# Letting the last routing steps of a top-2 mixture-of-experts kernel run on into the second expert block

## The chip, the cores and the metric

One core of one Trainium2 chip runs the kernel. The metric is the device time of one execution in microseconds; three runs are given, with their median. One further execution was taken with the hardware profiler.

## What is computed

Local attention over 64-token chunks (8 batches, 8 heads, 576 tokens, head size 64) gives 4608 tokens of 512 features. Each token then goes to the two best of eight experts, chosen by noisy logits:

```python
scores = scale * np.matmul(q_c, k_c.transpose(0, 1, 2, 4, 3))
attn = softmax(scores)                     # within each chunk of 64
x = heads_joined(np.matmul(attn, v_c))     # 4608 x 512
noisy_logits = x @ w_gate + np.log1p(np.exp(x @ w_noise)) * noise
top2_w = softmax of the two largest noisy logits
for e in range(8):
    h = np.maximum(x[mask] @ w1[e], 0.0)   # 512 -> 1024
    out[mask] += top2_w[mask, k, None] * (h @ w2[e])
```

All of it is in float32.

## The kernel before, in words

The program's order on each engine is the order in which the Python code issues instructions (`manual_schedule`); nothing reorders it. Each engine works through its own list and waits on semaphores where an operand is not ready.

**Attention and routing.** 36 tiles of 128 tokens go through attention (`attend`). Their results are written to `xbuf` in DRAM. The tiles form five groups, and for each group `route(g)` works out the two experts of every token, its place in each expert's list, and adds the group's share to the lists. `route` is a generator: it issues some instructions and yields, and `step_route(n)` lets it go on by n yields. So routing is woven between other work. `finish_route` (L614) issues all that is left at once.

For each of the eight tiles of a group, `route` builds comparison matrices (`gohp` on GpSimd, L557, and ScalarE, L558 and L559; `geq` and `grhs` on VectorE, L561 and L565 for the last group) and `place` (L547, matmuls on L549) sums their product into one PSUM bank. A tile's two `place` matmuls are called a pair here. Three buffers of each kind rotate, so a tile's matrices wait for the pair three tiles earlier. When all eight pairs are done, VectorE adds the bank to `acc` (L583), for the last group permutes the sums into the experts' order in four steps of two instructions (L596, L598), and `finish_lists` (L187 to L193, five instructions) makes the row numbers `lid`, the weights `lwt` and a float copy `lfl`. Then `gather(2)` (L601, issued on L219) fetches block 2's tokens with four indirect DMAs on GpSimd's queue.

The experts are put in an order by load; `order` (L522) holds it, and is known before the comparison matrices of the last group are begun. SP loads it into registers (L752) to fetch the later experts' weights (`w_load`).

**Experts.** Each expert's list is cut into three blocks, of 384, 384 and up to 448 tokens. `layer1(i)` makes eight slices f of the hidden layer; each slice is four steps d, and each step three matmuls of 128 x 384 (`three`, L284: hi*hi, hi*lo, lo*hi of float32 split into two parts). ScalarE then makes `hh` (L297) and VectorE `hl` (L298). `layer2(i)` makes, for each tile k of 128 tokens, eight times three matmuls; VectorE weighs the result (L304) and GpSimd adds it to `out` by an indirect DMA (L251). `x_tile` transposes a gathered tile for the next block (L267 on TensorE, hi on ScalarE L274, lo on VectorE L275).

Expert 0 is special: its first two blocks use lists of earlier groups (`EARLY`), so they can start before routing is done. Block 0's first layer still has attention's tail in it. Block 0's second layer takes two routing steps after each f, block 1's too (`hook2_r`), and `finish_route` stands between the two blocks. In block 1's second layer, after the first three matmuls, `pieces` (L197 to L207) turns `lfl` into indices of quarter rows: VectorE writes `xv` (L200), four matmuls (L204) spread the list, VectorE makes `piece` (L206). GpSimd then gathers block 3's tokens in twelve quarters (L239). `pg.close()` gives the routing buffers' memory back, and three pools take it.

Block 2's tiles are transposed within block 1's second layer, the first one after seven f of its first tile.

Of the kernel before, what the change touches and what calls it, by code (L numbers as in the profile page):

```python
# [51 lines left out]
def kernel(ctx, tc, qT, kT, vh, wgn, noise, w1, w2, out, caps=CAPS):  # L52
# [56 lines left out]
    def w_load(e, which, c):  # L109
        st = stage.tile([P, 1024], FT, name="st")  # L110
        staged[e, which, c] = st
        if which == 1:
            nc.sync.dma_start(st, w1v[ds(place[e], 1), c].rearrange("o j r f -> (o j) r f") if e else w1[e, c * P:(c + 1) * P, :])
        else:
            nc.sync.dma_start(st.rearrange("p (f n) -> p f n", f=2),
                              w2[ds(place[e], 1) if e else slice(0, 1), 2 * c * P:(2 * c + 2) * P, :]
                              .rearrange("o (f p) n -> p (o f) n", f=2))

    def w_split(e, which, c, half, eng=None):
        if half == 0:  # L120
            W[e, which, c] = (wpool.tile([P, 1024], FR, name=f"w{which}h{c}"),
                              wpool.tile([P, 1024], FR, name=f"w{which}l{c}"))
        hi, lo = W[e, which, c]
        st = staged[e, which, c]
        s = slice(half * 512, half * 512 + 512)
        nc.scalar.activation(hi[:, s], st[:, s], AF.Copy)
        (eng or nc.vector).tensor_sub(lo[:, s], st[:, s], hi[:, s].bitcast(FT))
# [44 lines left out]
    def bank(what, among=None):  # L172
        among = among or (BANKS if rot["l2"] < 6 else WIDE)[what]
        rot[what] += 1
        return PS[:, among[rot[what] % len(among)], :]
# [67 lines left out]
    def gathered(i, k):  # L243
        while quarters and quarters[0][0:2] <= (i, k):
            gather_some(1)
# [12 lines left out]
    def x_tile(i, k):  # L258
        e, b = BL[i]
        j, r = blocks[e][b][k]  # L260
        xh, xl = XH[i] = BX[i % 2]
        x = XG[e, j]
        s = slice(k * P, k * P + r)
        if i < NPE:
            src = bank("tr").rearrange("p (d n) -> p d n", d=ND)[:, :, 0:r]
            for d in range(ND):
                nc.tensor.transpose(src[:, d, :], x[0:r, d * P:(d + 1) * P], ident[0:r, 0:r])  # L267
            oh, ol = xh[:, :, s], xl[:, :, s]
        else:
            y = xy.tile([P, DM], FT, name="y")  # L270
            nc.vector.transpose(y[:, 0:4 * r], x[:, 0:4 * r])  # L271
            src = y[:, 0:4 * r].rearrange("p (t b c) -> p b t c", b=ND, c=32)
            oh, ol = (a[:, :, s].rearrange("p b (t c) -> p b t c", c=32) for a in (xh, xl))
        nc.scalar.activation(oh, src, AF.Copy)  # L274
        nc.vector.tensor_sub(ol, src, oh.bitcast(FT))  # L275

    def three(p, w, w_s, x, x_s, first, last, flip=False):

        (wh, wl), (xh, xl) = w, x
        for n, (a, b) in enumerate(((wh, xh), (wh, xl), (wl, xh)) if not flip else ((wh, xh), (wl, xh), (wh, xl))):  # L280
            a, b = a[w_s], b[x_s]
            if flip:
                a, b = b, a
            nc.tensor.matmul(p, a, b, start=first and n == 0, stop=last and n == 2)  # L284

    def layer1(i, hook, hook_d=lambda f, d: None):
        e, b = BL[i]
        n = sum(r for _, r in blocks[e][b])
        HT[i] = BH[i % 2]
        for f in range(NF):  # L290
            p = bank("l1", (0, 1) if i == 0 else None)[:, 0:n]
            for d in range(ND):
                three(p, W[e, 1, d], (slice(None), slice(f * P, (f + 1) * P)),
                      XH[i], (slice(None), d, slice(0, n)), d == 0, d == ND - 1)
                hook_d(f, d)
            hh, hl = HT[i][f]
            nc.scalar.activation(hh[:, 0:n], p, AF.Relu)  # L297
            nc.vector.scalar_tensor_tensor(hl[:, 0:n], p, 0.0, hh[:, 0:n].bitcast(FT), op0=OP.max, op1=OP.subtract)  # L298
            hook(f)
# [139 lines left out]
    def route(g):  # L439
# [73 lines left out]
        if g == LAST:  # L513

            key = gate.tile([P, NE], FT, name="gkey")
            V.tensor_copy(key, run8)
            V.memset(key[:, 0:1], float(2 ** 24))
            top = gate.tile([P, NE], FT, name="gtop")
            V.max(top, key)
            idx = gate.tile([P, NE], U32, name="gidx")  # L520
            V.max_index(idx, top, key)
            V.tensor_copy(order, idx[0:1])  # L522
            yield
            perm = gate.tile([P, NE, NE], FT, name="gperm")
            V.tensor_tensor(perm, e_row[:, None, :].to_broadcast([P, NE, NE]),
                            idx[:, :, None].to_broadcast([P, NE, NE]), OP.is_equal)
            accp = gate.tile([P, 2, NJ, NE], FT, name="gaccp")
            by_e = gate.tile([1, NE, NE], FT, name="gbye")
            V.tensor_tensor(by_e, perm[0:1].rearrange("p r e -> p e r"),
                            caprow[:, None, :].to_broadcast([1, NE, NE]), OP.mult)  # L530
            V.tensor_reduce(cape, by_e, AX.X, OP.add)
            yield
# [70 lines left out]
    routing = []  # L603

    def step_route(n):
        for _ in range(n):
            while routing:
                try:
                    next(routing[0])
                    break  # L610
                except StopIteration:
                    routing.pop(0)

    def finish_route():  # L614
        while routing:
            step_route(1)

    halves = [(c, h) for c in range(4) for h in range(2)]
# [79 lines left out]
    for i in range(NBL + 1):  # L698
        e, b = BL[i] if i < NBL else (NE, 0)
        if b == 1 % nb and e + 1 < NE and i > 1:  # L700
            for c in range(4):
                w_load(e + 1, 1, c)
        split2 = halves if i < NBL and (b == 1 % nb if e else b == 0) else []
        nxt = blocks[BL[i + 1][0]][BL[i + 1][1]] if i + 1 < NBL else []

        def turn_next(k):
            gathered(i + 1, k)
            x_tile(i + 1, k)
            ahead[0] -= 1

        def hook1(f):
            if i > 1 and b != 1 and f % 2 == 1 and f // 2 < len(nxt):
                turn_next(f // 2)
            if split2:
                w_split(e, 2, *split2[f])
            if i > 1:
                gather_some(1 + f % 2, HT[i][f][0])

        def hook2_f(k, f):
            if i > 1 and b == 1 and f % 4 == 1 and 2 * k + f // 4 < len(nxt):  # L720
                turn_next(2 * k + f // 4)
            if (k, f) == (0, 3):
                for q in split1:
                    w_split(split1_e, 1, *q)

        def hook2_r(k, f):
            hook2_f(k, f)
            step_route(2)
            if k + 1 < len(nxt) or i == 0:
                if f == 6 and k < len(nxt):  # L730
                    x_tile(i + 1, k)
            if i == 1 and (k, f) == (0, 0):
                pieces()
                gathered(3, 3)

        if 1 < i < NBL and i == 3:
            layer2(i - 1, hook2_f)
        if i < NBL:
            layer1(i, hook1, hook_tail if i == 0 else lambda f, d: None)
        split1 = halves if (i < NBL and b == nb - 1 and e + 1 < NE) else []  # L740
        split1_e = e + 1

        if i == 0:
            pa.close()
            block_bufs(1)
            OB[0] = pb.enter_context(tc.tile_pool(name="ob", bufs=4))
        if i == 0:
            zero_out(NT)
            layer2(0, hook2_r)
            finish_route()  # L750
            for r in range(1, NE):
                place[r] = nc.values_load(order[0:1, r:r + 1], engines=[mybir.EngineType.SP], min_val=0, max_val=NE - 1)  # L752
            for c in range(4):
                w_load(1, 1, c)
            pg.close()
            later_xg.append(pb.enter_context(tc.tile_pool(name="xg2", bufs=3)))
            xy = pb.enter_context(tc.tile_pool(name="xy", bufs=2))
            xv.append(pb.enter_context(tc.tile_pool(name="xv", bufs=1)))
        elif i == 1:
            layer2(1, hook2_r)  # L760
            x_tile(2, 3)
        elif i != 2 and i != 3:
            layer2(i - 1, hook2_f)
        if split1:
            for c in range(4):
                w_load(e + 1, 2, c)
# [132 lines left out]
```

## Time and profile before

| | |
|---|---|
| median of three runs | 1031.76 us (1029.02 to 1033.64) |
| profiled execution | 1033.37 us |
| its span | 1031.5 us |
| mean granted clock of TensorE | 0.981 of 2.4 GHz |
| TensorE / VectorE / ScalarE / GpSimd busy | 95% / 45% / 29% / 46% |

The span is the time from the first to the last instruction in the trace; the execution's own time also has what lies around it. A busy share is a mean over the whole span, in which attention, routing and the experts follow one another. Matmuls are pipelined: a duration of 0.34 us overlaps with the next matmul, so pitches are read from start to start.

### The profile page before, as it was taken

How to read it: one execution, taken by the hardware profiler on the slowest of the kernel's cores; microseconds unless marked ns; L12 is line 12 of the kernel's file. 1: busy time of each engine (PE TensorE's matmuls, PEld its weight loads, DVE VectorE, ACT ScalarE, POOL GpSimd, SP SyncE). 2: the span in 40 equal slices, each digit the busy share in tenths (PEclk: the TensorE clock that was granted, in tenths of full speed). 3: DMA queues.
4: the chain of work that ended last, by engine and by line, in shares of the span. 5: the costliest groups of instructions: out<-in, count | busy, mean ns of one | idle time of the engine just before them, and what ended most of it. 6: DMA issues, size and time to landing. Idle time of an engine off the chain costs nothing.

```text
span 1031.5 us, 17805 instructions
## 1 busy us (share of the span) xinstructions
PE 978.0 (95%) x7121; PEld 866.5 (84%) x7121; DVE 462.0 (45%) x1030; ACT 298.3 (29%) x617; POOL 479.6 (46%) x612
## 2 busy tenths in 40 slices
PE   6778978989999999999999999999999999999995
PEld 5666757887889889888988998899889998999884
DVE  5686665562525443344334432453245334533311
ACT  3565554331314221222222321232123222322100
POOL 1142422445675666157714772378428724801111
PEclk9989888999999999999999999999999999999998
DMA  9987891142442452345224423443334334412213
GB/s 370 402 326 256 280 388 51 41 113 67 95 105 82 95 133 57 58 101 138 54 53 104 130 60 49 103 136 61 51 111 122 77 54 106 135 19 31 31 21 42
DMA packets 51445, 121.48 MB, mean 118 GB/s; under 512 B 8272, under 2 KB 8528, under 8 KB 51360
## 3 DMA queue, kind: packets, MB, share of 16 engines
q0 software_dynamic: 19664, 38.69, 21.7%
q1 hardware_dynamic: 26512, 72.20, 19.3%
q10 hardware_dynamic: 5184, 9.44, 2.4%
q8 instruction: 56, 0.92, 0.4%
q14 instruction: 29, 0.24, 0.1%
HBM read 81.56 MB, written 38.73 MB: 117 GB/s over the span
## 4 chain that ended last, share of the span: by engine, by line
PE 89%; DVE 5%; DMA 2%; ACT 1%; issue 1%; POOL 0%; SPq 0%; ACTq 0%; DVEq 0%; POOLq 0%
PE PS L284 80%; PE PS L397 2%; PE PS L549 2%; PE PS L370 2%; DMA out<-zero 1%; PE PS L386 1%; PE PS L417 1%; DVE xs L409 1%; DVE mx L374 1%; DVE pr L379 1%; PE PS L435 1%; DMA xbuf<-xs 1%; PE PS L424 1%; DMA kb<-in_kT 0%; PE PS L267 0%
## 5 line engine op out<-in xcount | busy, mean ns | idle before, releaser
L239 POOL DMA_INDIRECT xg<-xbuf,piece x257 | 262.7, 1022 | 75.9 <-issue 70.4
L251 POOL DMA_INDIRECT out<-o,lid x77 | 122.2, 1587 | 316.7 <-DVE o L304 301.4
L284 PE MATMUL PS<-xh,w1h 128*128 128x384 f32 (+2 forms) x768 | 262.5, 342 | 1.9 <-DVE xl L275 1.4
L284 PE MATMUL PS<-xl,w1h 128*128 128x384 f32 (+2 forms) x768 | 260.8, 340 | 0.4 <-DVE xl L275 0.4
L284 PE MATMUL PS<-xh,w1l 128*128 128x384 f32 (+2 forms) x768 | 260.8, 340 | 0.0
L284 PE MATMUL PS<-w2h,hh 128*128 128x512 f32 x616 | 240.6, 391 | 0.0
L284 PE MATMUL PS<-w2h,hl 128*128 128x512 f32 x616 | 240.2, 390 | 0.0
L284 PE MATMUL PS<-w2l,hh 128*128 128x512 f32 x616 | 240.2, 390 | 0.0
L297 ACT ACTIVATE hh<-PS 128x384 fp32r<-128x384 f32 (+2 forms) x192 | 95.2, 496 | 474.5 <-PE PS L284 474.5
L298 DVE SCALAR_TENSOR_TENSOR hl<-PS,hh 128x384 fp32r<-128x384 f32 (+2 forms) x192 | 108.6, 566 | 193.0 <-ACT hh L297 193.0
L304 DVE TENSOR_SCALAR o<-PS,lwt 128x512 f32<-128x512 f32 x77 | 57.6, 749 | 242.6 <-PE PS L284 242.6
L284 PEld LDWEIGHTS PS<-xh,w1h 128*128 128x128 f32 x768 | 144.5, 188 | 5.4 <-DVE xl L275 1.7
L284 PEld LDWEIGHTS PS<-xl,w1h 128*128 128x128 f32 x768 | 144.6, 188 | 2.4 <-DVE xl L275 0.7
L284 PEld LDWEIGHTS PS<-xh,w1l 128*128 128x128 f32 x768 | 144.6, 188 | 0.9
L284 PEld LDWEIGHTS PS<-w2h,hl 128*128 128x128 f32 x616 | 112.9, 183 | 27.1
L284 PEld LDWEIGHTS PS<-w2l,hh 128*128 128x128 f32 x616 | 112.9, 183 | 26.1
L284 PEld LDWEIGHTS PS<-w2h,hh 128*128 128x128 f32 x616 | 112.9, 183 | 25.8
L274 ACT ACTIVATE xh<-y 128x512 fp32r<-128x512 f32 x67 | 41.2, 614 | 93.2 <-DVE y L271 93.2
L275 DVE TENSOR_TENSOR xl<-y,xh 128x512 fp32r<-128x512 f32 x67 | 45.1, 673 | 48.3 <-ACT xh L274 48.3
L557 POOL TENSOR_SCALAR gohp<-row_p,gpf 128x128 f32<-128x128 f32 x36 | 24.6, 715 | 66.4 <-DVE gpf L541 53.5
L397 PE MATMUL PS<-vb,pts 64*64 64x65 f32 x1152 | 29.4, 242 | 17.5 <-DVE xs L409 11.3
L271 DVE STREAM_TRANSPOSE y<-xg 128x512 f32<-128x512 f32 x67 | 45.6, 681 | 0.0
(130 smaller groups left out, 770.8 us busy)
## 6 DMA issues: line engine op xcount, KB each, us to landing
st<-in_w SPq DMA_DIRECT2D x64, 512.0 KB, 5.1
out<-zero SPq DMA_DIRECT2D x37, 256.0 KB, 4.6
vb<-in_vh SPq DMA_DIRECT2D x18, 520.0 KB, 3.9
qp<-in_qT SPq DMA_DIRECT2D x18, 512.0 KB, 7.2
kb<-in_kT SPq DMA_DIRECT2D x18, 512.0 KB, 9.0
xbuf<-xs ACTq DMA_DIRECT2D x36, 256.0 KB, 6.1
xg<-xbuf,piece POOLq DMA_INDIRECT x257, 2.6
out<-o,lid POOLq DMA_INDIRECT x77, 4.9
```

The lines of the kernel that those rows point to most:

```text
L239: nc.gpsimd.indirect_dma_start(out=XG[e, j][:, t * P:(t + 1) * P], out_offset=None, in_=xpieces, in_offset=bass.IndirectOffsetOnAxis(ap=pi ...
L251: s = nc.gpsimd.indirect_dma_start(out=out, out_offset=bass.IndirectOffsetOnAxis(ap=rows_of(i, j)[0:r], axis=0), in_=o[0:r], in_offset=Non ...
L271: nc.vector.transpose(y[:, 0:4 * r], x[:, 0:4 * r])
L274: nc.scalar.activation(oh, src, AF.Copy)
L275: nc.vector.tensor_sub(ol, src, oh.bitcast(FT))
L284: nc.tensor.matmul(p, a, b, start=first and n == 0, stop=last and n == 2)
L297: nc.scalar.activation(hh[:, 0:n], p, AF.Relu)
L298: nc.vector.scalar_tensor_tensor(hl[:, 0:n], p, 0.0, hh[:, 0:n].bitcast(FT), op0=OP.max, op1=OP.subtract)
L304: nc.vector.tensor_scalar(o[0:r], p[0:r], weights_of(i, j)[0:r], None, op0=OP.mult)
L370: nc.tensor.matmul(PS[s, h, o:o + 64], q[r, t % 2, hp, s], k[r, t % 2, hp, s], start=True, stop=True)
L397: nc.tensor.matmul(PS[s, 3 + h, hp * 65:hp * 65 + 65], PT[t][r, hp, s], v[r, t % 2, c, hp, :], start=True, stop=True)
L557: nc.gpsimd.tensor_scalar(ohp[:, 0], row_p, pf[:, 0, 0, r:r + 1], None, op0=OP.is_equal)
```

## The change

`finish_route` takes a condition. After block 0's second layer it now runs routing only until `order` has been issued (a list `ordered` notes that). `layer1(1)` takes one routing step after each of its 32 steps d (as `layer1` of every later block does, when nothing is left to route), and the rest of routing is issued before block 1's second layer. The pools that take the routing buffers' memory move with it.

```diff
             V.tensor_copy(order, idx[0:1])
+            ordered.append(g)
             yield
...
-    def finish_route():
-        while routing:
+    ordered = []
+
+    def finish_route(until=lambda: not routing):
+        while not until():
             step_route(1)
...
         if i < NBL:
-            layer1(i, hook1, hook_tail if i == 0 else lambda f, d: None)
+            layer1(i, hook1, hook_tail if i == 0 else lambda f, d: step_route(1))
...
         if i == 0:
             zero_out(NT)
             layer2(0, hook2_r)
-            finish_route()
+            finish_route(lambda: ordered)
             for r in range(1, NE):
                 place[r] = nc.values_load(order[0:1, r:r + 1], engines=[mybir.EngineType.SP], min_val=0, max_val=NE - 1)
             for c in range(4):
                 w_load(1, 1, c)
+        elif i == 1:
+            finish_route()
             pg.close()
             later_xg.append(pb.enter_context(tc.tile_pool(name="xg2", bufs=3)))
             xy = pb.enter_context(tc.tile_pool(name="xy", bufs=2))
             xv.append(pb.enter_context(tc.tile_pool(name="xv", bufs=1)))
-        elif i == 1:
             layer2(1, hook2_r)
```

The lists of GpSimd and SP are unchanged. On TensorE, at the border of block 0's second layer (`w2h`, `hh`, `hl`) and block 1's first (`xh`, `xl`, `w1h`, `w1l`), it stood before:

```order
L284 MATMUL PS<-w2h_3073,hh_2635 128x512
L284 MATMUL PS<-w2l_3074,hh_2635 128x512
L284 MATMUL PS<-w2h_3073,hl_2636 128x512
L549 MATMUL PS<-grhs,gohp 128x160 x16
L284 MATMUL PS<-xh_3122,w1h_702 128x384
L284 MATMUL PS<-xl_3123,w1h_702 128x384
L284 MATMUL PS<-xh_3122,w1l_703 128x384
```

and in the changed kernel, whose lines behind the change are numbered one to four higher:

```order
L284 MATMUL PS<-w2h_3073,hh_2635 128x512
L284 MATMUL PS<-w2l_3074,hh_2635 128x512
L284 MATMUL PS<-w2h_3073,hl_2636 128x512
L284 MATMUL PS<-xh_3122,w1h_702 128x384
L284 MATMUL PS<-xl_3123,w1h_702 128x384
L284 MATMUL PS<-xh_3122,w1l_703 128x384
L550 MATMUL PS<-grhs,gohp 128x160 x2
```

The sixteen routing matmuls have left the border; the first pair stands behind block 1's first step.

Also on TensorE, at the other end of block 1's first layer in the changed kernel (`hh_3124` and `hl_3125` are its second layer's operands; `lfl`, `xv` is the `pieces` matmul):

```order
L550 MATMUL PS<-grhs,gohp 128x160 x2
L284 MATMUL PS<-xh_3122,w1h_1111 128x384
L284 MATMUL PS<-xl_3123,w1h_1111 128x384
L284 MATMUL PS<-xh_3122,w1l_1112 128x384
L284 MATMUL PS<-xh_3122,w1h_1355 128x384
L284 MATMUL PS<-xl_3123,w1h_1355 128x384
L284 MATMUL PS<-xh_3122,w1l_1356 128x384
L550 MATMUL PS<-grhs,gohp 128x160 x2
L284 MATMUL PS<-w2h_2775,hh_3124 128x512
L284 MATMUL PS<-w2l_2776,hh_3124 128x512
L284 MATMUL PS<-w2h_2775,hl_3125 128x512
L204 MATMUL PS<-lfl,xv 128x80 x4
```

The seventh and the eighth pair are the two seen here. The eighth stands behind the whole first layer; three matmuls lie between it and `pieces`, where before the whole first layer lay between.

On VectorE, at block 1's last `hl` in the changed kernel:

```order
L298 SCALAR_TENSOR_TENSOR hl_3137<-PS,hh_3136 128x384
L298 SCALAR_TENSOR_TENSOR hl_3139<-PS,hh_3138 128x384
L584 TENSOR_TENSOR acc<-acc,PS 128x160
L597 TENSOR_TENSOR grhs<-acc,gperm 128x320
L599 TENSOR_REDUCE gaccp<-grhs 128x40
```

Three more repeats of the last two rows, the five instructions of `finish_lists` and `xv` (L200) follow. The fourteen instructions from `acc` to `lid` stood ahead of block 1's first `hl` before.

## Rows read from the trace of the kernel before

**Rows 1.** The page, busy us, share of the span, instructions of each engine.

```profile
PE 978.0 (95%) x7121; PEld 866.5 (84%) x7121; DVE 462.0 (45%) x1030; ACT 298.3 (29%) x617; POOL 479.6 (46%) x612
```

**Rows 2.** The chain of waits, in order of time: start, us, what.

```profile
218.06 16.66 PE PS L284 x96
...
256.22 763.46 PE PS L284 x3815
```

**Rows 3.** TensorE's timeline from 208 us: start, us, instruction, [idle before <-releaser].

```profile
208.01 0.40 PE L284 MATMUL PS<-w2h,hl 128*128 128x512 f32 x1
...
213.63 4.43 PE L549 MATMUL PS<-grhs,gohp 128*128 128x160 f32 x20 [3.44 <-DVE geq L561]
...
218.07 0.34 PE L284 MATMUL PS<-xl,w1h 128*128 128x384 f32 x1
...
234.37 0.33 PE L284 MATMUL PS<-xh,w1l 128*128 128x384 f32 x1
...
236.30 1.09 PE L204 MATMUL PS<-lfl,xv 128*128 128x80 f32 x8 [0.90 <-DVE xv L200]
237.19 0.47 PE L284 MATMUL PS<-w2h,hh 128*128 128x512 f32 x1
...
241.38 0.60 PE L267 MATMUL PS<-ident,xg 128*128 128x128 f32 x4
```

**Rows 4.** ScalarE's and VectorE's timelines, block 1's third tile.

```profile
208.73 0.58 ACT L274 ACTIVATE xh<-PS 128x512 fp32r<-128x512 f32 x1
...
209.34 0.69 DVE L275 TENSOR_TENSOR xl<-PS,xh 128x512 fp32r<-128x512 f32 x1
```

**Rows 5.** TensorE's timeline in block 0's first layer, about one routing pair.

```profile
177.78 0.34 PE L284 MATMUL PS<-xh,w1l 128*128 128x384 f32 x1
...
178.85 0.34 PE L284 MATMUL PS<-xh,w1l 128*128 128x384 f32 x1
```

**Rows 6.** GpSimd's timeline, the last two comparison matrices.

```profile
215.23 1.90 POOL L557 TENSOR_SCALAR gohp<-row_p,gpf 128x128 f32<-128x128 f32 x2 [0.51 <-PE PS L549]
```

**Rows 7.** VectorE's timeline, from the sum to the operand of `pieces`.

```profile
218.09 0.32 DVE L583 TENSOR_TENSOR acc<-acc,PS 128x160 f32<-128x160 f32 x1 [1.44 <-PE PS L549]
...
223.36 1.01 DVE L298 SCALAR_TENSOR_TENSOR hl<-PS,hh 128x384 fp32r<-128x384 f32 x2
...
235.74 0.42 DVE L200 COPY xv<-ident 128x512 f32<-128x512 f32 x1
```

**Rows 8.** Windows: us, busy us of PE, PEld, DVE, ACT, POOL, PEclk, DMA share, GB/s.

```profile
138.00:138.50 0.50, 0.50 (x19) 0.47 (x23) 0.36 (x4) 0.08 (x1) 0.00 (x0) 0.60 1.05 397
...
144.50:145.00 0.50, 0.50 (x12) 0.38 (x6) 0.20 (x1) 0.22 (x1) 0.00 (x0) 0.57 1.08 410
...
165.00:165.50 0.50, 0.50 (x20) 0.49 (x24) 0.46 (x4) 0.00 (x0) 0.00 (x0) 0.91 0.00 0
...
168.50:169.00 0.50, 0.50 (x5) 0.50 (x4) 0.17 (x1) 0.00 (x0) 0.50 (x2) 0.68 0.00 0
...
213.00:213.25 0.25, 0.00 (x0) 0.00 (x0) 0.25 (x2) 0.00 (x0) 0.25 (x2) 0.90 2.17 139
...
216.50:216.75 0.25, 0.25 (x3) 0.25 (x3) 0.16 (x1) 0.22 (x2) 0.25 (x1) 0.78 0.22 74
```

**Rows 9.** TensorE's timeline in the attention stage, two waits.

```profile
164.99 0.88 PE L397 MATMUL PS<-vb,pts 64*64 64x65 f32 x24 [0.78 <-DVE xs L409]
...
173.30 1.06 PE L424 MATMUL PS<-xt,wg 128*32 128x512 f32 x8 [1.64 <-ACT xt L418]
```

**Rows 10.** GpSimd's timeline, block 2's first gather.

```profile
223.72 1.07 POOL L219 DMA_INDIRECT xg<-xbuf,lid  x1 [6.59 <-DVE lid L193]
```

**Rows 11.** By line: landing of L219's ten gathers, then of L251's scatters, 200 to 215 us.

```profile
DMA to landing us min/median/max: 3.4/7.3/8.0
...
DMA to landing us min/median/max: 4.8/7.6/10.3
```

**Rows 12.** A window behind block 1's first layer, columns as in rows 8.

```profile
238.50:239.00 0.50, 0.50 (x4) 0.41 (x3) 0.00 (x0) 0.00 (x0) 0.28 (x1) 1.00 0.10 41
```

## The prediction

> **What bounds the kernel now.** I read the page's busy shares first: TensorE is busy 95% of the span, so time is won only where it stands still or does work it need not do [rows 1]. Next the chain of waits: from 256.2 us to 1019.7 us it is one piece of TensorE matmuls [rows 2]. Whatever happens up to 256 us is therefore shifted one to one into the end, and nothing behind it gives it back. The change acts between 208 and 256 us, so I read that stretch instruction by instruction on TensorE [rows 3], and beside it ScalarE, VectorE and GpSimd.
>
> The reader should see two waits there. The last layer-two matmul of block 0 starts at 208.01, but the second layer-one matmul of block 1 only at 218.07: 16 routing matmuls (32 passes on the engine) stand between, and they wait for VectorE and GpSimd, 3.44 us at one point [rows 3]. Then block 1's 96 layer-one matmuls run at 16.66/96 = 0.1735 us each [rows 2]. Three layer-two matmuls later comes the `pieces` matmul (L204), after a wait of only 0.90 us [rows 3].
>
> **The change, step by step.** The profiled execution took 1033.37 us (span 1031.5), 1.6 us more than the median 1031.76; I work out differences in the trace and add them to the median.
>
> *Start of block 1.* The routing matmuls are no longer ahead of it. What is late next is the block's own input: of its third tile, ScalarE has the hi part at 208.73 + 0.58 = 209.31, VectorE the lo part at 209.34 + 0.69 = 210.03 [rows 4]. The order of both engines up to there is the same, so these times stay. The first matmul can go at 209.4 and the second at 210.07, which went at 218.07 [rows 3]: **8.0 us earlier**.
>
> *Routing matmuls inside block 1.* They still cost TensorE. In block 0 one pair stretched three matmul starts to 178.85 − 177.78 = 1.07 us, against 3 × 0.1735 = 0.52 [rows 5]: 0.55 us a pair. Seven pairs lie before the last layer-one matmul, 3.85 us; the eighth, 0.55, right behind it. Their operands have slack: the pairs are mostly five steps apart, 2.6 us of matmuls, and the slowest operand takes GpSimd 1.90/2 = 0.95 us [rows 6]. So the last layer-one matmul starts at 234.37 − 8.0 + 3.85 = 230.22.
>
> *What is queued behind.* The sum `acc` (L583) needs the eighth pair, so the fourteen VectorE instructions from `acc` to the list `lid` now come after block 1's last `hl`, where before they ran under block 1's matmuls. Before, VectorE was free for its next instruction 235.74 − 234.37 = 1.37 us after the last layer-one matmul's start [rows 3, 7]; so `acc` goes at 231.59 (the eighth pair is done sooner). From `acc` to the instruction behind `lid` it took 223.36 − 218.09 = 5.27 us [rows 7]; `xv` goes at 236.86. From `xv` to L204 it took 236.30 − 235.74 = 0.56 [rows 3, 7]; L204 goes at 237.42, **1.1 us later than before**. The same from TensorE's side: it was done with what stands before L204 at 236.30 − 0.90 = 235.40, and now is at 235.40 − 8.0 + 4.4 = 231.8; it stands for 5.6 us. The wait in front of block 1 has become a wait inside its second layer: 8.0 won, 4.4 paid for pairs, 4.7 for the longer wait.
>
> *The clock.* The granted clock fell to 0.50 (1.2 GHz) at 213.2, within the wait; work came back at 213.63 and full clock at 216.6 [rows 3, 8]. These 3.0 us fell on routing matmuls that waited anyway. Behind the new wait, half clock falls on matmuls that are all on the path. In another place it lasted from 165.4 to 168.8, 3.8 us after work came back at 164.99 [rows 8, 9]. Half of 3.0 to 3.8 us is 1.5 to 1.9; I take **1.7**, the middle. The Trainium skill, "TensorE: Matmul & The Clock Gate" (section "HAM oscillation — how this bites in real kernels"), prices throttled time at a half too and warns against loops that starve TensorE between bursts; by it, the change is a worse place for a wait, and the sum would gain the same 1.7.
>
> For the first, short wait (1.1 us, one matmul, 0.5 us) the trace has both answers: about the 0.78 us wait that ended at 164.99 the clock fell, about the 1.64 us wait that ended at 173.30 it did not [rows 8, 9]. Bounds 0 and 1.7; I take 0, since the longer of the two waits, nearest in length, had none.
>
> *The gather of block 2* is issued 223.72 − 218.09 = 5.63 us behind `acc` [rows 7, 10], at 237.2. The transpose that needs it stood 4.19 us behind 237.19 [rows 3], so now at 237.42 + 0.89 (L204) + 4.19 + 1.7 = 244.2. Such gathers landed after 3.4 to 8.0 us [rows 11]: ready at 240.6 to 245.2, a cost of 0 to 1.0. I take 0: the slow landings ran beside other traffic, and the weight load beside this one ebbs by 238.5 (41 GB/s) [rows 12]. By the Trainium skill, "DMA: Bandwidth & Descriptors" (section "Anatomy of one DMA — SWDGE (gpsimd) path"), 256 KB takes an estimated 2.6 us by its fit, and the cost is 0 as well; by the slowest row it would be 1.0.
>
> *Further on.* GpSimd's gathers of block 3, twelve quarters behind these, come about 4 us later, near 257.5 instead of 253.5; block 3's first tile is wanted in the second step of block 2's first layer, past 262. I price that at 0, and as much as the gather's 1.0 if the cover is short. The order of experts and its weight load hang on instructions that have not moved: 0.
>
> **Sum:** −8.0 + 4.4 + 4.7 + 1.7 = **+2.8 us**, so 1031.76 + 2.8 = **1034.6 us**.
>
> **Rivals.** *A, the list chain does not hold TensorE.* L204 at 231.8 against 236.30 gives −4.5: 1027.3. For it: before, the wait at L204 was only 0.90. Against it: there 96 matmuls covered the chain, now three do; its 5.27 us would have to shrink below 1. *B, the clock decides, on the slow side.* It falls at both waits, and stays as long as from 138.1 to 144.9, 6.8 us [rows 8]. Price 3.4 us each: +1.1 + 6.8 = +7.9: 1039.7. It makes the kernel measurably slower from (5.2 − 1.1) × 2 = 8.2 us of work at half clock on. For it: such a stretch is in the trace. Against it: that lay in the attention stage, among many short waits, and dense matmuls follow here. *C, the gather lands late*, as late as the longest of the scatters nearby, 10.3 us [rows 11]: 247.5, 3.3 us past need, +6.1: 1037.9. *D, the change does little of what it says*, if routing were done by the end of block 0's second layer. The order excludes it: 16 matmuls move.
>
> **How the numbers follow.** The forecast has 0.76 (with its bounds +1.1 to +5.5: the 1.7 of the short wait and the 1.0 of the gather on top), A 0.09, B 0.08, C 0.07. A measurement tells this kernel from no change beyond 0.5%, 5.2 us. The forecast is within that but for its upper tip, 0.01; A is within by its number, 0.02 of it beyond; B and C are slower by more than that, 0.11 of their 0.15, the rest within as the runs spread. So faster 0.02, same 0.86, slower 0.12. The range: low, the forecast without clock loss, +1.1, less the runs' half spread of 2.3: 1030.5; high, the forecast's upper bound with 0.8 of spread, which takes in C: 1038.1. A and B stay outside, 0.17.
>
> **What would show it.** Right: TensorE idles under 2 us ahead of block 1's first layer; its 96 matmuls take near 21 us with seven pairs between; a wait of 5 to 6 us stands before L204, released by VectorE's `xv`; the clock reads 0.50 behind it for 3 to 4 us; block 2's first layer begins some 3 us later than now. Wrong: a wait at L204 of under 2 us (A), routing matmuls that wait inside block 1, over 1 us of wait at block 2's transposes (C), or half clock right after 210 as well (B).

## The result

The changed kernel takes **1035.83 us** (median of 22 runs, 1031.47 to 1039.09), the kernel before on the same chip 1032.96 us (22 runs, 1028.76 to 1034.85). The ratio is 1.0031, 95% interval 1.0019 to 1.0043: 3.2 us more, by the interval 2.0 to 4.4; forecast were 2.8 more. The forecast time, 1034.6 us, is 1.2 us lower, because it starts from the median of three runs, 1031.76. By the bound set ahead, 0.5%, this is no change, though the interval excludes a ratio of 1.

The profiled execution of the changed kernel took 1033.30 us with a span of 1031.5, as long as the profiled one of before. All that stands ahead of the change took 3.0 us less in it: the last layer-two matmul of block 0 starts at 205.01, in the trace of before at 208.01 [rows 3]. That is not the change's doing: the traces of the kernel before have this place at 208.01, 204.53 (`c_before`) and 206.80 (`g_before_late`), those of the changed kernel at 205.01 and 207.54 (`c_after`). Yet the long piece of the chain starts at 256.23, before at 256.22 [rows 2]. The stretch between the two, which holds all of the change, grew from 48.21 to 51.22 us, by **3.0 us**. Three profiled executions were slow ones, of 1124.81 us (`e3_same_chip`), 2479.98 us (`g_after_late`) and 1401.43 us (`c2_before`, the kernel before once more, its only run), and are not read.

Busy time hardly moved; the page, columns as in [rows 1]:

```profile
PE 976.3 (95%) x7121; PEld 864.7 (84%) x7121; DVE 461.8 (45%) x1030; ACT 298.4 (29%) x617; POOL 481.4 (47%) x612
```

TensorE's timeline of the changed kernel, columns as in [rows 3] (L550 is the routing pair, L549 before):

```profile
205.01 0.40 PE L284 MATMUL PS<-w2h,hl 128*128 128x512 f32 x1
206.36 0.44 PE L284 MATMUL PS<-xh,w1h 128*128 128x384 f32 x1 [0.96 <-ACT xh L274]
207.09 0.44 PE L284 MATMUL PS<-xl,w1h 128*128 128x384 f32 x1 [0.28 <-DVE xl L275]
207.54 0.70 PE L550 MATMUL PS<-grhs,gohp 128*128 128x160 f32 x4
...
227.32 0.33 PE L284 MATMUL PS<-xh,w1l 128*128 128x384 f32 x1
227.49 0.70 PE L550 MATMUL PS<-grhs,gohp 128*128 128x160 f32 x4
...
228.50 0.39 PE L284 MATMUL PS<-w2h,hl 128*128 128x512 f32 x1
234.50 1.96 PE L204 MATMUL PS<-lfl,xv 128*128 128x80 f32 x8 [5.61 <-DVE xv L200]
236.20 0.77 PE L284 MATMUL PS<-w2h,hh 128*128 128x512 f32 x1
...
241.38 0.60 PE L267 MATMUL PS<-ident,xg 128*128 128x128 f32 x4
```

At the border only 1.24 us of wait are left, for block 1's own input. No pair waits inside the block. The stall now stands in front of L204, 5.61 us long. Between 200 and 300 us, these are all of TensorE's waits (for what: us in total, times, longest):

```profile
PE PS L204 <- DVE xv L200: 5.6, 1, 5.6
PE PS L284 <- ACT xh L274: 1.4, 2, 1.0
PE PS L284 <- DVE xl L275: 0.7, 2, 0.4
```

The chain of waits, which answers to [rows 2], goes through VectorE's list where before it had gone through `grhs` (L565) and the sixteen matmuls:

```profile
207.71 0.54 PE PS L550 x4
208.25 2.60 PE PS L284 x15
...
228.21 0.56 DVE hl L298
234.50 1.96 PE PS L204 x8
236.47 5.08 PE PS L284 x18
...
256.23 763.46 PE PS L284 x3815
```

VectorE's timeline shows what TensorE waits for in those 5.61 us; it answers to [rows 7]. From `acc` to `xv` VectorE goes from one instruction to the next without a wait:

```profile
228.21 0.56 DVE L298 SCALAR_TENSOR_TENSOR hl<-PS,hh 128x384 fp32r<-128x384 f32 x1 [2.07 <-ACT hh L297]
228.69 0.31 DVE L584 TENSOR_TENSOR acc<-acc,PS 128x160 f32<-128x160 f32 x1
...
233.82 0.20 DVE L193 CAST lid<-lfl 128x80 int32<-128x80 f32 x1
233.94 0.42 DVE L200 COPY xv<-ident 128x512 f32<-128x512 f32 x1
```

Windows about the two waits, columns as in [rows 8]. The clock keeps 1.00 through the short wait; within the long one it falls to 0.50, and it is back soon after 238:

```profile
206.25:206.50 0.25, 0.14 (x1) 0.14 (x1) 0.16 (x1) 0.06 (x1) 0.00 (x0) 1.00 0.01 0
...
231.00:231.50 0.50, 0.00 (x0) 0.00 (x0) 0.47 (x2) 0.00 (x0) 0.00 (x0) 0.99 0.22 90
231.50:232.00 0.50, 0.00 (x0) 0.00 (x0) 0.50 (x2) 0.00 (x0) 0.00 (x0) 0.50 0.12 49
234.50:235.00 0.50, 0.50 (x3) 0.50 (x3) 0.00 (x0) 0.00 (x0) 0.50 (x1) 0.50 0.00 0
...
238.00:238.50 0.50, 0.50 (x3) 0.41 (x2) 0.00 (x0) 0.00 (x0) 0.31 (x1) 0.68 0.77 311
238.50:239.00 0.50, 0.50 (x4) 0.40 (x3) 0.00 (x0) 0.00 (x0) 0.50 (x1) 1.00 0.60 123
```

And block 2's gather on GpSimd, with the landing of its four parts, which answer to [rows 10, 11]; the second landing is that of the same four before the change:

```profile
234.30 1.07 POOL L219 DMA_INDIRECT xg<-xbuf,lid  x1 [12.68 <-DVE lid L193]
```

```profile
DMA to landing us min/median/max: 3.2/3.4/3.8
...
DMA to landing us min/median/max: 7.6/7.7/8.0
```

The first tile was there by 234.30 + 3.8 = 238.1 at the latest, and is wanted at 241.38, so 3.3 us were to spare.

### The profile page after: what moved, and what is told of

It reads as the page before. It is cut to its first block, busy times and chain, and to the rows that moved or that the text cites. A ratio compares the mean times of both kernels' runs of the same rounds, so it can differ in the third digit from the quotient of the medians.

```text
span 1031.5 us, 17796 instructions
## 1 busy us (share of the span) xinstructions
PE 976.3 (95%) x7121; PEld 864.7 (84%) x7121; DVE 461.8 (45%) x1030; ACT 298.4 (29%) x617; POOL 481.4 (47%) x612
## 4 chain that ended last, share of the span: by engine, by line
PE 88%; DVE 5%; DMA 2%; ACT 1%; SPq 1%; issue 1%; DVEq 0%; ACTq 0%
PE PS L284 80%; PE PS L550 1%; PE PS L397 1%; PE PS L370 1%; DMA out<-zero 1%; PE PS L386 1%; SPq L629 1%; PE PS L417 1%; DVE mx L374 1%; DVE xs L409 1%; DVE pr L379 1%; PE PS L424 1%; DMA xbuf<-xs 1%; PE PS L435 1%; DMA kb<-in_kT 0%
## 5 line engine op out<-in xcount | busy, mean ns | idle before, releaser
L251 POOL DMA_INDIRECT out<-o,lid x77 | 122.2, 1587 | 314.1 <-DVE o L304 298.8
```

The lines of the kernel that those rows point to most:

```text
L251: s = nc.gpsimd.indirect_dma_start(out=out, out_offset=bass.IndirectOffsetOnAxis(ap=rows_of(i, j)[0:r], axis=0), in_=o[0:r], in_offset=Non ...
```

## The experiments

The theory: the time went into two things at the second place, VectorE's list chain that three layer-two matmuls cannot cover (4.7 us) and the half clock behind it (1.7 us); the pairs cost 4.4 us wherever they stand; the 8.0 us at the border are truly won. The rivals: the list chain is not what holds the kernel; the clock's price is not on the path; the border's gain is lost again later.

The first chip is that of the result. `e1` to `e4` ran on a second one, the `c` runs, `e3_same_chip` and `e5` on a third, the `g` runs on a fourth, each with its own runs of the kernel before (medians 1041.21, 1042.23 and 1032.94 us), so ratios stand against those. (It is not on record whether the fourth is another chip than the first.) The changed kernel itself did not run on the second chip. Edits are to the changed kernel unless another is named.

**`e1_two_steps`: routing done sooner.** Two routing steps after each step d, so that routing ends half-way through block 1's first layer and its matmuls cover the list again:

```diff
-            layer1(i, hook1, hook_tail if i == 0 else lambda f, d: step_route(1))
+            layer1(i, hook1, hook_tail if i == 0 else lambda f, d: step_route(2))
```

> The changed kernel with two routing steps instead of one after each step of block 1's first layer, so that the eighth pair stands about half way through that layer and half of the layer's matmuls cover the list chain on VectorE. Theory (the loss is the chain's place, not the pairs): the wait before L204 falls from 5.6 us to about 1 us, the clock stays at 1.00 there, the 8.0 us at the start of block 1 stay and the pairs cost 4.4 us, so 3.6 us less than the kernel before (ratio 0.9965) and some 6.5 us less than the changed kernel. Rival (routing inside block 1 costs as such: pairs wait for GpSimd and VectorE there, and hl comes late): waits of L550 inside block 1 of over 2 us in sum, ratio 1.000 to 1.003.

Measured: 1037.12 us, ratio 0.9965 (0.9948 to 0.9981). TensorE's timeline:

```profile
208.66 0.40 PE L284 MATMUL PS<-w2h,hl 128*128 128x512 f32 x1
...
233.89 1.09 PE L204 MATMUL PS<-lfl,xv 128*128 128x80 f32 x8 [0.90 <-DVE xv L200]
238.97 0.60 PE L267 MATMUL PS<-ident,xg 128*128 128x128 f32 x4
```

The wait is 0.90 us as before the change, L204 takes 1.09 us as at full clock. From block 0's last layer-two matmul (208.66) to L267 are 30.31 us; in the traces of the first chip 33.37 before the change and 36.37 after it. So the same matmuls, in another place, turn +3 into −3 us, and the ratio, taken on one chip, says −3.6. The list chain's place decides; that the border's gain is real is shown with it.

**`e2_pieces_later`: the list wanted one tile later.**

```diff
-            if i == 1 and (k, f) == (0, 0):
+            if i == 1 and (k, f) == (1, 0):
                 pieces()
                 gathered(3, 3)
```

> The changed kernel with the pieces matmul and the gathers of block 3 moved by one tile, behind the first matmuls of the second tile of block 1's second layer, some 5.5 us of matmuls later. Theory (the whole list chain is late, the next to wait for it is block 2's gather): the wait before L204 goes, but TensorE then waits about 5 us at block 2's first transposes (L267), for a gather that is issued at the same time as in the changed kernel and lands 3.2 to 3.8 us later; half clock follows there; 0.5 to 1 us less than the changed kernel, still 2 us above the kernel before (ratio 1.002). Rival (only the pieces matmul stands in the way): no wait at L267 over 1 us, ratio 0.9965.

Measured: 1042.90 us, ratio 1.0017 (1.0001 to 1.0033).

```profile
240.88 1.12 PE L267 MATMUL PS<-ident,xg 128*128 128x128 f32 x4 [4.72 <-DMA xg<-xbuf,lid]
...
244.55 1.09 PE L204 MATMUL PS<-lfl,xv 128*128 128x80 f32 x8 [0.18 <-DVE xv L200]
```

The wait at L204 is down to 0.18 us, and block 2's transposes wait 4.72 us for the gather that hangs on the same list. Half clock follows there, as expected: the four transposes take 1.12 us instead of 0.60. To shift the first consumer only brings out the second: it is the list that must come sooner.

**`e3_dummy_matmuls`: the wait kept, TensorE kept busy in it.** Forty matmuls that nobody reads, into free columns of the bank of `pieces`:

```diff
             if i == 1 and (k, f) == (0, 0):
+                for _ in range(40):
+                    nc.tensor.matmul(PS[:, 7, 320:512], W[0, 1, 0][0][:, 0:P], XH[1][0][:, 0, 0:192], start=True, stop=True)
                 pieces()
```

> The changed kernel with forty matmuls of 128x192 more, whose result nobody reads, just before the pieces matmul, where TensorE stands for 5.6 us. It adds work and takes none away; only the granted clock can gain. Theory (1.7 to 1.8 us of the loss is half clock behind the wait): the forty take 4 to 5 us, L204 starts as before relative to the last layer-one matmul, the clock reads 1.00 behind it, L204's eight passes take 0.9 to 1.1 us instead of 1.96, and the kernel is 1.8 us faster than the changed one, 1.2 us above the kernel before (ratio 1.001). Rival (the clock is no part of it): the same time as the changed kernel, ratio 1.003.

Measured: 1043.56 us, ratio 1.0034 (1.0019 to 1.0048). The clock read 1.00 about L204, which took 1.09 us, yet the time was not reduced: a miss. In its trace TensorE stood later on for something new, ahead of block 2 (waits between 200 and 300 us, two of them), and there the clock did fall, from 256.7 to 266.9 us (a window of it, columns as in [rows 8]):

```profile
PE PS L267 <- issue: 4.1, 4, 1.2
PE PS L284 <- ACT xh L274: 3.9, 2, 3.0
```

```profile
264.00:264.50 0.50, 0.50 (x2) 0.46 (x3) 0.00 (x0) 0.00 (x0) 0.50 (x1) 0.50 0.00 0
```

**`e4_three_steps_before`: routing done sooner from the other side.** Three steps after each f of block 0's second layer:

```diff
-            step_route(2)
+            step_route(3 if i == 0 else 2)
```

> The changed kernel with three routing steps instead of two after each f of block 0's second layer, one step in block 1's first layer as in the change. Six pairs then stand in block 0's second layer and two in block 1's first, the list chain behind block 1's second slice. Theory: pairs cost the same 4.4 us wherever they stand among matmuls, the chain is covered, L204 waits about 1 us; the start of block 1 waits less for its third tile, since ScalarE and VectorE are no longer busy with the first three comparison matrices then: 3.6 to 5.2 us less than the kernel before (ratio 0.995 to 0.9965). Rival (routing this early has no slack): TensorE waits for L550 or for the rank matmuls (L495, L497) inside block 0's second layer by 2 to 4 us, ratio 0.998 to 1.001.

Measured: 1037.95 us, ratio 0.9969 (0.9957 to 0.9981).

```profile
206.17 0.81 PE L550 MATMUL PS<-grhs,gohp 128*128 128x160 f32 x4 [0.83 <-POOL gohp L558]
...
230.07 1.09 PE L204 MATMUL PS<-lfl,xv 128*128 128x80 f32 x8 [0.90 <-DVE xv L200]
```

One pair in block 0 waits 0.83 us for GpSimd; the wait at L204 is short again. The ratio lies between the theory's range and the rival's, next to the theory's. It gains much as e1 does: what counts is that routing is over early in block 1.

**`c_before` and `c_after`: both kernels again, on the third chip.**

> The kernel before, unchanged, once more with a profile, since the four profiles above come from another chip than the two of the prediction, and show ScalarE and VectorE late in block 1's second layer (waits of TensorE of 3 to 7 us for ScalarE's xh ahead of block 2's first layer) which neither of those two has. If that lateness belongs to the chip, it can stand here too, between 236 and 262 us; if it came from the experiments' edits, it does not. Ratio 1.000.

> The changed kernel, unchanged, once more with a profile on the same chip as c_before. From the end of block 0's second layer to L204's end it differs from c_before as in the first pair of profiles: 8.0 us earlier start, 4.4 us of pairs, a wait of 5 to 6 us at L204, half clock behind it. Ratio 1.003.

Measured: 1044.03 us, ratio 1.0022 (1.0002 to 1.0042), for the kernel before against itself, and 1042.68, ratio 1.0005 (0.9992 to 1.0017), for the changed one. The second is a miss: 1.003 was expected. And a ratio here can be off by 0.2%, a little more than its interval says, so a difference of 3 us is read from a trace rather than from one ratio. Locally the changed kernel does the same on this chip:

```profile
237.03 1.97 PE L204 MATMUL PS<-lfl,xv 128*128 128x80 f32 x8 [5.61 <-DVE xv L200]
```

Between the two traces of this chip, the start of block 1 gives −8.24, the seven pairs +3.94, the eighth and the list chain +5.24 and the half clock +1.78: +2.72 us from block 0's last layer-two matmul to L267.

But in this chip's trace of the *unchanged* kernel ScalarE is late for block 2's third tile, whose transposes started at 250.00:

```profile
255.47 0.87 ACT L274 ACTIVATE xh<-PS 128x512 fp32r<-128x512 f32 x2 [9.40 <-remote]
```

From the first L267 to the second matmul of block 2's first layer it takes 257.84 − 238.15 = 19.7 us here, 256.22 − 241.38 = 14.84 in the trace of before and 14.85 in that of the changed kernel on the first chip. All six traces of changed forms that were read on the second and the third chip have such a lateness, in other amounts: this stretch takes 19.6 us in e1, 20.7 in `c_after`, 22.7 in e3. A shift of 2 us ahead of it need not arrive behind it: from the second matmul of block 1 to L267, e3 needs 32.46 us and `c_after` 34.26, 1.8 more; in the stretch behind it e3 needs 2.0 more. (These are two executions on two chips, so this is a hint.)

Where the 2.72 us went on this chip, the two traces show. The first row is a wait on TensorE's timeline of `c_before` that `c_after` has not; the second is the last long piece of the chain of `c_before`, the third that of `c_after`:

```profile
319.72 0.45 PE L284 MATMUL PS<-xh,w1h 128*128 128x384 f32 x1 [1.60 <-ACT xh L274]
...
320.45 705.53 PE PS L284 x3527
...
264.55 765.05 PE PS L284 x3815
```

From block 0's last layer-two matmul (204.53 and 207.54) to the end of these pieces, `c_before` takes 821.45 us and `c_after` 822.06: +0.6, as the ratio of 1.0005 says. The stretch from L267 adds 1.0 to the 2.72, and behind it `c_before` needs 3.1 us more, 2.3 of them at this wait for a later block's input. On the first chip neither kernel has that wait.

**`e3_same_chip`: e3 beside `c_after`.**

> The kernel with the forty unread matmuls, on the same chip as c_before and c_after. Its first profile had the clock at 1.00 behind L204 and L204's eight passes at 0.89 us instead of 1.70, as the theory has it, but its time did not come down, and a wait of 3.0 us for xh and slow starts of the transposes stood behind. If these belong to the chip: from the end of layer one of block 1 to block 2's first layer this kernel takes 1.8 us less than c_after where neither has such a wait, and a ratio of 1.001 to 1.002 is expected here. If the half clock is worth nothing in time: the ratio of c_after, 1.003 or more, and the same span between these two places.

Measured: 1042.92 us, ratio 1.0003 (0.9991 to 1.0015), equal to `c_after`, whose own ratio was not the 1.003 that both forecasts started from. On a chip with that lateness the clock's price does not show in the time.

**`e5_two_steps_and_borders`: a version that takes the remaining waits too.** e1, with `x_tile` for block 1 after five f instead of seven, and `pieces` two f later:

```diff
-                if f == 6 and k < len(nxt):
+                if f == (4 if i == 0 else 6) and k < len(nxt):
                     x_tile(i + 1, k)
-            if i == 1 and (k, f) == (0, 0):
+            if i == 1 and (k, f) == (0, 2):
...
-            layer1(i, hook1, hook_tail if i == 0 else lambda f, d: step_route(1))
+            layer1(i, hook1, hook_tail if i == 0 else lambda f, d: step_route(2))
```

> The kernel of e1_two_steps with the two waits that it has left taken away: block 1's tiles are transposed two f earlier in block 0's second layer (so that ScalarE and VectorE have done the third one before the first comparison matrices of the last group), and the pieces matmul stands two f later. Theory: the 1.2 us ahead of block 1's first layer and the 0.9 us before L204 go, 2.1 us on top of 3.6: ratio 0.9945. Rival (both waits are taken over by what stands behind, the first routing pair and block 2's gather): waits of the same sum at L550 or L267, ratio 0.9965 as without it.

Measured: 1035.71 us against 1042.23, ratio 0.9935 (0.9916 to 0.9953), the best of all.

```profile
208.10 0.40 PE L284 MATMUL PS<-w2h,hl 128*128 128x512 f32 x1
...
231.98 1.01 PE L204 MATMUL PS<-lfl,xv 128*128 128x80 f32 x8
235.64 0.60 PE L267 MATMUL PS<-ident,xg 128*128 128x128 f32 x4
```

L204 waits for nothing, and neither does the border: 235.64 − 208.10 = 27.54 us from block 0's last layer-two matmul to L267, against 33.62 in `c_before` on the same chip: 6.1 less, where the theory has 5.7.

**`g_before_late`, `g_after_late`, `g_after_dummies`: the lateness and the clock apart.** To see whether GpSimd's gathers cause the lateness, block 3's twelve quarters are issued later, in the kernel before, in the changed kernel, and in the changed kernel with e3's dummies:

```diff
             if i == 1 and (k, f) == (0, 0):
                 pieces()
+            if i == 1 and (k, f) == (2, 7):
                 gathered(3, 3)
```

> The kernel before, with block 3's twelve quarter gathers issued behind the last f of block 1's second layer instead of behind its first step. Theory G (the lateness of ScalarE, VectorE and TensorE there comes from these gathers running beside them): the stretch from block 2's first transposes to the second matmul of block 2's first layer shrinks to 14.9 us, as on the first chip, and the kernel gains up to 5 us on a chip that shows the lateness (ratio 0.995 to 0.998). Rival (the lateness has nothing to do with the gathers): the stretch stays as long as in the kernel before on this chip, ratio 1.000 to 1.002.

> The changed kernel with the same move of the gathers. Where the lateness is gone, it should stand 2.8 us behind the kernel before with that move (0.0027 in the ratio), by the sum of the prediction; where the lateness hides part of a shift, less.

> As the run before it, with forty unread matmuls (128 x 192, into free columns of the bank that the pieces matmul uses) ahead of the pieces matmul, so that TensorE does not stand idle while VectorE makes the list. If the clock behind the wait costs 1.7 to 1.8 us and nothing later swallows them, the ratio is 0.0017 lower than that of the run before it; if the clock's price is not on the path, both are equal within 0.0007.

Measured, against 1032.94 us: 1032.44, ratio 0.9994 (0.9979 to 1.0009); 1036.01, ratio 1.0026 (1.0012 to 1.0040); 1033.64, ratio 1.0007 (0.9995 to 1.0020). The fourth chip has not got the lateness (`g_before_late` takes 255.28 − 240.44 = 14.84 us in that stretch, as the kernel before did on the first chip), so its cause was not put to the test, and the move alone is worth nothing. The changed kernel stands 0.0032, 3.3 us, behind the kernel before with the same move; 2.8 were forecast. And the dummies lower the ratio by 0.0019, 2.0 us, where nothing later swallows it. That is no more than a ratio can be off by; the trace shows that it is the clock, which reads 1.00 from 200 to 270 us (a window of it stands last, columns as in [rows 8]):

```profile
202.66 0.40 PE L284 MATMUL PS<-w2h,hl 128*128 128x512 f32 x1
...
226.71 4.71 PE L737 MATMUL PS<-xh,w1h 128*128 128x192 f32 x40 [0.16 <-DVE acc L584]
232.16 1.09 PE L204 MATMUL PS<-lfl,xv 128*128 128x80 f32 x8 [0.74 <-DVE xv L200]
...
237.26 0.60 PE L267 MATMUL PS<-ident,xg 128*128 128x128 f32 x4
...
252.11 0.47 PE L284 MATMUL PS<-xl,w1h 128*128 128x448 f32 x1 [0.37 <-DVE xl L275]
```

```profile
233.00:233.50 0.50, 0.50 (x5) 0.45 (x4) 0.21 (x1) 0.00 (x0) 0.20 (x2) 1.00 0.12 33
```

The operand of L204 comes no sooner, but L204 takes 1.09 us in place of 1.96, and the whole stretch, 252.11 − 202.66 = 49.45 us, is 1.8 shorter than the 51.22 of the changed kernel on the first chip.

## Why the prediction was right

Taken from block 0's last layer-two matmul, so that the 3.0 us that stand ahead of it drop out, the terms of the sum came out so:

| term | forecast | measured | from |
|---|---|---|---|
| border of block 1 | −8.0 | −7.98 | (207.09 − 205.01) − (218.07 − 208.01) |
| seven pairs within block 1 | +3.85 | +3.93 | (227.32 − 207.09) − (234.37 − 218.07) |
| eighth pair and list chain, to L204 | +5.25 | +5.25 | (234.50 − 227.32) − (236.30 − 234.37) |
| half clock, L204 to L267 | +1.7 | +1.80 | (241.38 − 234.50) − (241.38 − 236.30) |
| from there to the long piece | 0 | 0.0 | 14.85 − 14.84 |
| sum | +2.8 | +3.0 | |

- *Start of block 1.* The next late thing was the block's own input, as said, and the first wait was 0.96 + 0.28 = 1.24 us.
- *Pairs.* 0.54 us each in the chain, 3.93/7 = 0.56 by the starts, forecast 0.55, and none waits, so the operands had the slack that [rows 6] promised.
- *What is queued behind.* VectorE's fourteen instructions ran right behind the last `hl`, and the forecast wait of 5.6 us was 5.61. Rival A needed this chain to be no bound; e1 and e4 show that it is, since they shorten the wait to 0.90 us and gain 3.6 and 3.2 us by nothing but routing that ends sooner. e2 shows the reach of it: `pieces` and the gather hang on the same list.
- *The clock.* It fell where forecast and stood at half for 3.8 us of work (234.50 to about 238.3); half of that is 1.9, the measured price 1.80. `g_after_dummies` shows it to be the clock: with the wait still there but TensorE busy, it is gone. What the Trainium skill says in "TensorE: Matmul & The Clock Gate" (section "HAM oscillation — how this bites in real kernels"), that throttled time costs half of itself, agrees with these rows. The prediction's upper 3.8 us is a misreading, which here did no harm: it counts from the return of work at 164.99, while at half clock that row stood from 165.4 to 168.8, 3.4 us. Rival B, a fall at both waits, did not come: the clock stayed at 1.00 about the short wait. That the price there was 0 was chosen between two rows that disagree, so this term was partly luck.
- *The gather of block 2.* Taken at 0, was 0: it landed 3.2 to 3.8 us after issue, not 7.6 to 8.0 as before, when the weight load ran beside it. The Trainium skill's "DMA: Bandwidth & Descriptors" (section "Anatomy of one DMA — SWDGE (gpsimd) path") gives an estimated 2.6 us by its fit; the measurement stands 0.6 to 1.2 us above, and decides. Rival C, 10.3 us, was far off.
- *Further on.* GpSimd's gathers of block 3 ended at 254.1 us rather than 253.4, in a trace that runs 3.0 us ahead, so 3.7 us later; forecast were 4, and nobody waited for them.
- *The sum against the runs.* 2.8 forecast, 3.0 in the trace, 3.2 by the ratio, and 3.3 on the fourth chip with the gathers moved. On the third chip the same kernel gave 1.0005: the local picture is the same, +2.72, and in the two traces read it is taken up behind it, for the most part by a wait that the kernel before had and the changed one had not. So the sentence that nothing behind 256 us gives a shift back holds on the first chip and not on the third. Why that wait stands in the one trace only, and whether it does so in every execution, is not shown.

## What to carry to other kernels

When work is moved off a border, follow what its last product is wanted for: here the matmuls could run anywhere, but the list at their end has two early consumers, and the wait went to the first of them, where it also drew the clock down over matmuls on the path. The same edit with the work finished half a block sooner gains what this one loses, so ask not only whether work can overlap but when its chain must end. Moving one consumer back is no cure while another hangs on the same product. And a shift that the trace shows in one place is followed to the end of the chain, on each chip: on the third one a later wait in the other kernel made up for most of it.

## What was not expected of the hardware

On two of the chips (medians of the kernel before 1041 to 1042 us, against 1033 on the others) ScalarE or TensorE is late at some point between 245 and 262 us without a releaser in this kernel: "remote", "issue" or "another core or an unknown queue" in the traces. The stretch from L267 grows by 4.7 to 7.8 us by it (19.5 in e4 to 22.7 in e3, against 14.84; e2, whose stretch holds L204 too, is left out). In each of these traces the clock falls there as well, and stands at 0.50 over the first matmuls of block 2, in `c_before` until 262.0 us. The unchanged kernel shows the lateness too:

```profile
256.40 0.74 PE L284 MATMUL PS<-xh,w1h 128*128 128x448 f32 x1 [4.71 <-ACT xh L274]
```

The DMA engines are then busy with GpSimd's scatters to `out` (L251): 0.86 of their time from 252.0 to 256.4 us in `c_before`. But so they are in the kernel before on the first chip, 0.96 from 256.5 to 262.0 us, where nothing is late. No run on the second or the third chip kept both the gathers and the scatters away from this place, so the cause stays open.

A wait of 0.96 us, with one matmul and 0.28 us more behind it, left the clock at 1.00 here, whereas about one of 0.78 us in the attention stage it had fallen [rows 8, 9]. About the 1.64 us wait that ended at 173.30 [rows 9] it had not; these are two windows of before, columns as in [rows 8]:

```profile
172.50:173.00 0.50, 0.00 (x0) 0.00 (x0) 0.36 (x2) 0.38 (x2) 0.06 (x1) 1.00 0.00 0
...
174.00:174.50 0.50, 0.50 (x5) 0.20 (x2) 0.00 (x0) 0.07 (x1) 0.00 (x0) 1.00 0.15 33
```

So these rows give no length of a wait from which on it falls.
